# Score matmuls over 40 instead of 26 columns, and loads tied to the mixing, in talking-heads attention with an MLP

## The chip, the cores and the metric

One core of one Trainium2 chip runs the whole program. The metric is the device time of one execution in microseconds. The kernel before took 931.24 us, the median of three runs (928.26 to 932.08).

## The reference

Attention whose heads are mixed before and after the softmax, then a two-layer MLP with a PReLU (4 batches, 12 heads, 448 positions, 64 per head; 768 to 2048 to 768). q, k, v, w_pre and w_post are float32; the MLP's weights are float64.

```python
scores = scale * np.matmul(q, k.transpose(0, 1, 3, 2))
scores = np.einsum('bhij,hg->bgij', scores, w_pre)
scores = scores - np.max(scores, axis=-1, keepdims=True)
attn = np.exp(scores)
attn = attn / (np.sum(attn, axis=-1, keepdims=True) + 1e-09)
attn = np.einsum('bhij,hg->bgij', attn, w_post)
x = np.matmul(attn, v)                       # then [B*S, H*D]
h = x @ w_in
g = np.maximum(h, 0.0) + alpha * np.minimum(h, 0.0)
out = g @ w_out
```

## The kernel before

**Tiles.** Each batch's 448 query positions are cut into four chunks, three of 120 rows and one of 90 (CHUNKS, line 27); there are 16 chunks. The scores of one chunk and one pair of heads are a group Q (function qk, line 278): for two heads, hf, and two halves of the rows, ch, a matmul with at most 64 query rows as the stationary operand and k's 448 positions as the moving one. The first half has 64 columns of q, the second the rest: 56 in a 120-row chunk, 26 in a 90-row one (line 285). Each float32 matmul is two TensorE instructions in the trace, so a group Q is eight. ACT or DVE copies the result to st (qk_out, line 295).

The head mixing needs heads on partitions. A relay (line 303) is a DMA inside the on-chip memory that gathers 10 query rows times 12 heads of st into one of eight sr buffers. Two relays make a mixing block m (mix, line 308; 90 blocks in all): M mixes on TensorE, R takes the maximum on DVE (line 318), E the exponential on ACT (line 325), N the reciprocal and the scaled weights on DVE (lines 331 to 335), P the second mixing with a transpose on TensorE (line 347), A copies to at (line 359). When a chunk's blocks are done, pv (line 362) multiplies by v, xe takes the result's two parts and store_x writes them to DRAM for the MLP.

Meanwhile the raw float64 weights of the first three blocks of the MLP are fetched (fetch, line 406; six fetches of 768 KB) and rounded by seven DVE operations each (round_f64, lines 57 to 63). The MLP (lines 534 to 594) follows, two matmul layers of TensorE work, and converts the rest of its weights on the way.

**Order.** The program's order in the attention phase is written by a planner, plan (line 66). It knows every step with an engine, a duration, a priority on the scale of the mixing blocks, steps that must come before it, buffers that it takes and gives back, and sometimes an earliest time (at). It walks through them as a list scheduler would, and the instructions are written in the order of the times it assigns (line 641). A predecessor in the planner thus adds no wait to the program; it moves the instruction's place in its engine's queue. The waits in the program come from the data and the buffers alone.

**Queues.** The loads of q (LQ, load_q, line 257), k (LK, load_k, line 249; a third of a batch's k each), v (LV, load_v, line 266) and raw weights (F) are issued by GpSimd, except for the first chunk's. Relays go in turn to SP and GpSimd. GpSimd executes its queue in order, so a load stands behind the relays written before it and ahead of those after it. There are three q buffers, four for thirds of k, one for v, two for raw weights; in the planner LQ takes a buffer when one is free, and the bare earliest times of 18 and 20 hold back v and the raw weights at the start. The steps that the planner places, and their priorities, are lines 82 to 145; its costs stand in line 42 (a group Q is 0.82 whatever the chunk).

Of the kernel before, what the change touches and what calls it, by code (L numbers as in the profile page):

```python
# [31 lines left out]
NP = H // 2  # L32
# [3 lines left out]
RAHEAD = 3  # L36
# [2 lines left out]
FGROUPS = [[0, 1, 2], [3, 4, 5], [6, 7, 8], [9, 10, 11], [12, 13, 14, 15]]  # L39
NPRE = 3  # L40
NXS = 3
COST = {"Q": 0.82, "M": 0.82, "P": 1.0, "V": 2.15, "U": 3.7, "mode": 0.15, "R": 1.09, "E": 1.37, "N": 0.68}
HOP, DRAIN = 0.07, 0.2
LOOK = 0.3
# [21 lines left out]
def plan(groups, first, chunk_list):  # L66
# [5 lines left out]
    def op(name, engs, prio, preds=(), acq=(), rel=(), at=0.0):  # L72
        if isinstance(engs, tuple):
            engs = [engs]
        ops[name] = (engs, prio, list(dict.fromkeys(preds)), acq, rel, at)

    pe = lambda kind, mode="q": ("PE", COST[kind], DRAIN, mode)
    act = lambda d: ("ACT", d, HOP, "")
    dve = lambda d: ("DVE", d, HOP, "")
    dma = lambda d, l=3.0: ("DMA", d, l, "")  # L80

    for ci, (b, c) in enumerate(chunk_list):
        op(("LQ", ci), dma(1.0) if ci >= 2 else dma(0.0, 0.0), first[max(ci - 1, 0)] / 2 - RAHEAD - 5, acq=(("q", ci),))
        for p in range(NP):
            n = ci * NP + p
            prio = (n - NP) * 0.92 - 1
            op(("Q", ci, p), pe("Q"), prio, [("LQ", ci), ("LK", b, p // 2)], (("slot", (ci, p)),) + ((("st", ci),) if p == 0 else ()),
               ((("q", ci),) if p == NP - 1 else ()) + ((("k", b, p // 2),) if c == len(CHUNKS) - 1 and p % 2 else ()),
               at=5.5 + 1.1 * p if ci == 0 else 10.0)
            op(("S", ci, p), [act(0.92), dve(1.09)], prio, [("Q", ci, p)], rel=(("slot", (ci, p)),))  # L90
    for b in range(B):
        f4 = first[4 * b]
        for kk in range(NP // 2):
            op(("LK", b, kk), dma(1.2) if b else dma(0.0, 0.0), f4 / 2 - RAHEAD - 11 + kk, acq=(("k", b, kk),))
        op(("LV", b), dma(3.0), f4 / 2 + (4 if b else 0), acq=(("v", b),), at=18.0)
    for n, (ci, r) in enumerate(groups):
        op(("L", n), dma(0.8, 4.0), n / 2 - 1 - RAHEAD, [("S", ci, p) for p in range(NP)], (("sr", n),),
           (("st", ci),) if n + 1 == first[ci + 1] else ())
# [1 line left out]
    for m in range(NB):  # L100
        op(("M", m), pe("M"), m - 1, [("L", 2 * m), ("L", 2 * m + 1)], (("slot", m),), (("sr", 2 * m), ("sr", 2 * m + 1)), at=12.0)
        op(("R", m), dve(COST["R"]), m - 1, [("M", m)])
        op(("E", m), act(COST["E"]), m, [("R", m)], (("e", m),), (("slot", m),))
        op(("N", m), dve(COST["N"]), m + 1, [("E", m)], (("r", m),))
        op(("P", m), pe("P"), m + 2, [("N", m)], (("pa", m),), (("e", m), ("r", m)))
        for g in range(2):
            ci = groups[2 * m + g][0]
            op(("A", m, g), [act(0.52), dve(0.63)], m + 1.7, [("P", m)],
               (("at", ci),) if 2 * m + g == first[ci] else (), (("pa", m),))
    for ci, (b, c) in enumerate(chunk_list):  # L110
        lb = (first[ci + 1] - 1) // 2
        mine = [("A",) + divmod(n, 2) for n in range(first[ci], first[ci + 1])]
        for hx in range(2):
            pr = lb + 3.3 + 1.5 * hx
# [5 lines left out]
    nh = 2 * NPRE  # L120
    for i in range(nh):
        pr = 6 + 11 * i
        op(("F", i), dma(2.0, 4.0), pr - 6, acq=(("cr", i),), at=20.0)
        for j in range(7):
            op(("C", i, j), dve((0.57, 0.57, 0.57, 0.96, 0.57, 0.96, 0.96)[j]), pr + 1.3 * j,
               [("C", i, j - 1) if j else ("F", i)] + ([("C", i - 1, 6)] if i and not j else []),
               (("ct", i),) if j == 1 else (), (("cr", i),) if j == 5 else ())
        op(("WS", i), dma(1.0), pr + 10, [("C", i, 6)], rel=(("ct", i),))
# [3 lines left out]
    for f in range(NPRE):  # L132
        op(("LW", f), dma(2.0, 6.0), NB - 9 + f, [("WS", i) for i in range(nh)], (("cr", ("w", f)),))
        for x in range(2):
            pr = NB - 3 + 1.2 * f + 0.6 * x
# [3 lines left out]
    for u in range(2):  # L139
# [6 lines left out]

    cap = {"slot": 3, "st": NXS, "sr": 2 * (RAHEAD + 1), "e": LAG + 1, "r": LAG + 1, "pa": 1, "at": 2, "q": 3, "k": 4, "v": 1,
           "xe": 2, "cr": 2, "ct": 2}
# [14 lines left out]
    while ready:  # L163
        best = None
        for n in ready:
            engs, prio, preds, acq, rel, at = ops[n]
# [3 lines left out]
            for e, d, l, md in engs:  # L170
                d += COST["mode"] if e == "PE" and md != mode else 0.0
                t = max(t0, idle[e])
# [26 lines left out]
def talking_heads_prelu(ctx: ExitStack, tc: tile.TileContext, q, k, v, w_pre, w_post, mask, w_in, w_out, alpha, out):  # L199
    nc = tc.nc  # L200
# [5 lines left out]
    groups, first = [], []  # L206
# [40 lines left out]
    k_t, q_t, v_t, s_t, a_t = {}, {}, {}, {}, {}  # L247
# [9 lines left out]
    def load_q(ci, dmas=None):  # L257
        b, c = chunk_list[ci]
        c0, cn = CHUNKS[c]
        q_t[ci] = qp.tile([128, NP * CW], F32, tag="q", name=f"q{ci}")  # L260
        for hf in range(2):
            dma = dmas[hf] if dmas else nc.gpsimd
            dma.dma_start(out=q_t[ci][64 * hf:64 * hf + 64, :NP * cn],
                          in_=q[b, :, QOFF[c] + NP * hf * cn:QOFF[c] + NP * (hf + 1) * cn])
# [10 lines left out]
    def slot_tile(i, name):  # L275
        return ps.tile([128, 2, 512], F32, tag=f"b{i}", name=name)

    def qk(ci, p, slot):
        b, c = chunk_list[ci]
        cn = CHUNKS[c][1]  # L280
        ps = slot_tile(slot, f"s{ci}_{p}")
        for hf in range(2):
            for ch in range(2):
                r = slice(64 * hf, 64 * hf + 64)
                i0, i1 = 64 * ch, min(64 * ch + 64, cn)
                nc.tensor.matmul(ps[i0:i1, hf, :S], q_t[ci][r, p * cn + i0:p * cn + i1], k_t[b, p // 2][r, p % 2, :],  # L286
                                 start=True, stop=True)
        u_t["qk", ci, p] = ps
# [132 lines left out]
    with tc.manual_schedule():  # L421
        start = p1r.enter_context(tc.tile_pool(name="start", bufs=1, side="right"))
        hw = (nc.sync, nc.scalar)
        load_q(0, hw)
        load_k(0, 0, ((0, 1), (1, 2)), hw)
        load_k(0, 1, dmas=hw)
# [20 lines left out]
        for i, w in enumerate((w_pre, w_post)):  # L447
            for p in ((SR0, 64), (0, 64))[i]:
                nc.gpsimd.dma_start(out=mask_sb[p:p + HP, i], in_=mask[:HP, :HI, :])
                nc.gpsimd.dma_start(out=wb[p:p + HP, i, :],  # L450
                                    in_=w.rearrange("(o h) g -> o h g", o=1).to_broadcast([HI, H, H]))
        load_q(1)
        nc.gpsimd.dma_start(out=alpha_sb, in_=alpha)
        nc.vector.tensor_scalar(out=oma, in0=alpha_sb, scalar1=-1.0, scalar2=1.0, op0=ALU.mult, op1=ALU.add)
# [8 lines left out]
            op=ALU.mult,  # L463
# [14 lines left out]
        def load_x(bl, i):  # L478
            x_t[bl] = s_tile(i, f"x{len(x_log)}_{bl}").rearrange("p (t c) s -> p t c s", t=2)
            x_log.append(bl)  # L480
            x_in[i] = bl
            for t in range(2):
                nc.sync.dma_start(out=x_t[bl][:, t], in_=x2[t, :, :, bl * S:(bl + 1) * S].rearrange("c p i -> p c i"))
# [132 lines left out]
        def emit(n, e, got):  # L616
            kind, a = n[0], n[1:]
            if (kind == "LQ" and a[0] < 2) or (kind == "LK" and a[0] == 0):
                return
            if kind == "Q":  # L620
                qk(*a, got["slot"])
                if a[1] == 0:
                    s_t[a[0]] = s_tile(got["st"], f"st{a[0]}")
            elif kind in ("S", "A", "XH", "XL"):
                {"S": qk_out, "A": post_out, "XH": lambda c, x, e: pv_out(c, x, 0, e),
                 "XL": lambda c, x, e: pv_out(c, x, 1, e)}[kind](*a, e)
            elif kind == "L":
                relay_q(a[0], got["sr"])
            elif kind == "E":
                exp(a[0], 0)  # L630
                exp(a[0], 1)
            elif kind in ("M", "V", "U"):
                {"M": mix, "V": pv, "U": l1}[kind](*a, got["slot"])
            elif kind == "LX":
                load_x(a[0], got["st"])
            else:
                {"LQ": load_q, "LK": load_k, "LV": load_v, "R": rmax, "N": norm, "P": post, "W": store_x, "F": fetch,
                 "C": conv_op, "WS": store_w, "OPEN": turn, "LW": load_pre, "G": act_op,
                 "HH": lambda f, x: split_pre(f, x, 0), "HL": lambda f, x: split_pre(f, x, 1)}[kind](*a)

        for _, _, n, e, got in plan(groups, first, chunk_list):
            emit(n, e, got)
# [23 lines left out]
        def prefetch(u):  # L666
            nxt = []
            for _, bl, _ in units[u:]:
                if bl not in nxt:
                    nxt.append(bl)  # L670
                if len(nxt) == NXS:
                    break
            for bl in nxt[1:]:
                if bl not in x_in.values():
                    free = [i for i in range(NXS) if x_in.get(i) not in nxt]
                    load_x(bl, free[0])
# [54 lines left out]
```

## Time and profile before

| | |
|---|---|
| median of three runs | 931.24 us |
| the profiled execution | 935.73 us, span 934.0 us |
| TensorE matmuls | 878.8 us busy, 94% |
| DVE | 578.4 us, 62% |
| ACT | 343.5 us, 37% |
| GpSimd | 110.6 us, 12% |
| attention phase | about 0 to 440 us |
| MLP | about 440 to 934 us |

The engine shares are means over two phases with different limits. The chain that ended last is followed back from the last instruction; its pieces tell at each moment which engine or transfer the end waited for. A line like "64*26 64x448" names a stationary operand of 64 partitions and 26 columns and a moving operand of 448 columns.

### The profile page before, as it was taken

How to read it: one execution, taken by the hardware profiler on the slowest of the kernel's cores; microseconds unless marked ns; L12 is line 12 of the kernel's file. 1: busy time of each engine (PE TensorE's matmuls, PEld its weight loads, DVE VectorE, ACT ScalarE, POOL GpSimd, SP SyncE). 2: the span in 40 equal slices, each digit the busy share in tenths (PEclk: the TensorE clock that was granted, in tenths of full speed). 3: DMA queues.
4: the chain of work that ended last, by engine and by line, in shares of the span. 5: the costliest groups of instructions: out<-in, count | busy, mean ns of one | idle time of the engine just before them, and what ended most of it. 6: DMA issues, size and time to landing. Idle time of an engine off the chain costs nothing.

```text
span 934.0 us, 23852 instructions
## 1 busy us (share of the span) xinstructions
PE 878.8 (94%) x10380; PEld 665.5 (71%) x10380; DVE 578.4 (62%) x1023; ACT 343.5 (37%) x718; POOL 110.6 (12%) x194
## 2 busy tenths in 40 slices
PE   8589998999889997998899999999999999979998
PEld 3354565456553665456899999999999999869997
DVE  4475787569854886456455566667666763873332
ACT  3453765357643675346222222121212211211110
POOL 5122223222311222000000000000000000000000
PEclk9799999999999999999999999999999999989999
DMA  7666677566754469754831242025012511232111
GB/s 194 188 191 154 185 220 205 157 197 181 217 156 129 137 204 251 225 175 131 259 151 34 68 151 70 34 68 185 35 34 68 186 34 35 68 106 106 60 60 59
DMA packets 70974, 125.36 MB, mean 134 GB/s; under 512 B 32614, under 2 KB 59246, under 8 KB 70870
## 3 DMA queue, kind: packets, MB, share of 16 engines
q0 software_dynamic: 15344, 59.22, 21.8%
q1 hardware_dynamic: 54866, 63.33, 21.4%
q8 instruction: 81, 1.33, 0.6%
q10 hardware_dynamic: 660, 1.30, 0.5%
q14 instruction: 23, 0.19, 0.1%
HBM read 66.16 MB, written 18.92 MB: 91 GB/s over the span
## 4 chain that ended last, share of the span: by engine, by line
PE 82%; DVE 6%; DMA 6%; ACT 3%; issue 2%; SPq 0%; POOL 0%; ACTq 0%; DVEq 0%; POOLq 0%
PE h L541 25%; PE acc L579 24%; PE s L286 13%; PE x L369 8%; PE pa L347 7%; PE m L313 7%; DMA sr<-st 5%; DVE at L359 1%; DVE nm L318 1%; ACT e L325 1%; DVE ao L591 1%; ACT st L299 1%; ACT at L359 1%; DMA k<-in_k_dram 1%; DVE ct L60 0%
## 5 line engine op out<-in xcount | busy, mean ns | idle before, releaser
L541 PE MATMUL h<-x,w 128*128 128x448 f32 x1152 | 250.5, 370 | 6.4 <-ACT w L504 6.3
L579 PE MATMUL acc<-g,w 128*128 128x448 f32 x1152 | 245.6, 366 | 2.0 <-DVE t L556 1.4
L541 PEld LDWEIGHTS h<-x,w 128*128 128x128 f32 x1152 | 217.3, 189 | 28.8 <-ACT w L504 6.7
L579 PEld LDWEIGHTS acc<-g,w 128*128 128x128 f32 x1152 | 216.1, 188 | 21.7 <-DVE t L556 1.7
L286 PE MATMUL s<-k,q 64*64 64x448 f32 (+2 forms) x768 | 159.9, 555 | 1.9 <-ACT st L299 0.6
L347 PEld LDWEIGHTS pa<-r,e 64*64 64x64 f32 x5040 | 100.0, 136 | 58.7 <-issue 33.2
L556 DVE SCALAR_TENSOR_TENSOR t<-t,oma,h 128x448 f32<-128x448 f32 x64 | 43.5, 680 | 157.8 <-ACT t L554 157.8
L554 ACT ACTIVATE t<-h 128x448 f32<-128x448 f32 x64 | 34.9, 545 | 268.1 <-PE h L541 268.1
L325 ACT ACTIVATE e<-m,nm 128x448 f32<-128x448 f32 x180 | 112.7, 636 | 31.6 <-DVE nm L318 20.4
L318 DVE TENSOR_REDUCE nm<-m 128x2 f32<-128x896 f32 x90 | 97.6, 1085 | 36.1 <-PE m L313 35.7
L347 PE MATMUL pa<-r,e 64*64 64x60 f32 x5040 | 105.8, 223 | 14.6 <-issue 9.4
L313 PE MATMUL m<-sr,wk 64*64 64x448 f32 x720 | 97.7, 566 | 21.6 <-DMA sr<-st 18.4
L286 PEld LDWEIGHTS s<-k,q 64*64 64x64 f32 (+2 forms) x768 | 37.2, 128 | 78.2 <-issue 65.0
L369 PEld LDWEIGHTS x<-at,v 128*64 128x64 f32 x1536 | 75.6, 138 | 20.1 <-issue 6.6
L359 DVE COPY at<-pa 128x480 f32<-128x480 f32 x83 | 53.8, 656 | 54.8 <-ACT at L359 30.4
L306 POOL DMA_DIRECT2D sr<-st x89 | 53.2, 600 | 286.2 <-PE m L313 189.6
L369 PE MATMUL x<-at,v 128*64 128x120 f32 (+1 forms) x1536 | 82.5, 264 | 3.7 <-DVE at L359 1.4
L299 ACT COPY st<-s 120x896 f32<-120x896 f32 (+1 forms) x65 | 58.6, 906 | 67.7 <-PE s L286 61.2
L359 ACT COPY at<-pa 128x480 f32<-128x480 f32 x97 | 53.8, 570 | 69.7 <-PE pa L347 55.1
L313 PEld LDWEIGHTS m<-sr,wk 64*64 64x64 f32 (+1 forms) x720 | 24.9, 134 | 55.1 <-DMA sr<-st 22.2
L558 ACT CAST g<-t 128x448 fp32r<-128x448 f32 x64 | 36.3, 567 | 53.9 <-DVE t L556 53.9
L591 DVE TENSOR_TENSOR ao<-ao,acc 128x448 f32<-128x448 f32 x96 | 52.7, 613 | 1.7 <-PE acc L579 1.7
(49 smaller groups left out, 522.3 us busy)
## 6 DMA issues: line engine op xcount, KB each, us to landing
x<-x SPq DMA_DIRECT2D x16, 1344.0 KB
sr<-st SPq DMA_DIRECT2D x89, 210.0 KB
sr<-st POOLq DMA_DIRECT2D x89, 210.0 KB, 4.8
cr<-in_w_in_dram POOLq DMA_DIRECT2D x16, 768.0 KB, 4.7
cr<-in_w_out_dram POOLq DMA_DIRECT2D x16, 768.0 KB, 4.6
x<-xe SPq DMA_DIRECT2D x48, 180.0 KB
out_dram<-ao SPq DMA_DIRECT2D x24, 224.0 KB
v<-in_v_dram POOLq DMA_DIRECT2D x4, 1152.0 KB, 9.3
```

The costliest lines, as they stand in the source:

```text
L286: nc.tensor.matmul(ps[i0:i1, hf, :S], q_t[ci][r, p * cn + i0:p * cn + i1], k_t[b, p // 2][r, p % 2, :], start=True, stop=True)
L299: copy(dst[:cn, p], u_t.pop(("qk", ci, p))[:cn, :, :S])
L306: dma.dma_start(out=sr_t[n][SR0:SR0 + GP], in_=s_t[ci][r:CHUNKS[chunk_list[ci][1]][1]:CHUNKS[chunk_list[ci][1]][1] // GI])
L313: nc.tensor.matmul(ps[hf:hf + 64, u, :S], wk[r, :], g[r, :], start=True, stop=True)
L318: nc.vector.tensor_reduce(out=nm, in_=m_t[m][:, :, :S], axis=AX.X, op=ALU.max, negate=True)
L325: nc.scalar.activation(out=e_t[m][:, u], in_=m_t[m][:, u, :S], func=AF.Exp, bias=nm_t[m][:, u:u + 1], scale=1.0, accum_out=se_t[m][:, u:u ...
L347: nc.tensor.matmul(dst[:, :, HI * u:HI * u + HI], e[h, u, 64 * jb:64 * jb + 64], r[h, u].rearrange("p (h i) -> p h i", h=H), start=True, s ...
L359: copy_on[eng](dst, pa[:, g, :NS * GP].rearrange("p (s i) -> p s i", i=GI))
L369: nc.tensor.matmul(ps[64 * t:64 * t + 64, 0, cl * CW:cl * CW + cn], v_t[b][:, s, h * D:(h + 1) * D], a_t[ci][:, s, h, :cn], start=(s == 0) ...
L541: nc.tensor.matmul(ps[:, :S], w[:, tw, cc * 128:(cc + 1) * 128], x[:, tx, cc, :], start=(i == 0), stop=(i == 3 * NCC - 1))
L579: nc.tensor.matmul(accs[c][:, :S], w[:, tw, c * 128:(c + 1) * 128], g[:, tg], start=(f == fs[0] and i == 0), stop=(f == fs[-1] and i == 2))
L591: nc.vector.tensor_tensor(acc_sb[c, bl], acc_sb[c, bl], accs[c][:, :S], ALU.add)
```

## The change

The second half of a 90-row chunk's score matmuls takes 40 columns of q instead of 26 (MIN_M): rows 64 to 103 of the result instead of 64 to 89. The extra 14 columns are the next pair's first ones, and for the last pair columns of the q tile that no load fills, so a memset on GpSimd sets them to zero before the load. Rows 90 to 103 of the result are not read.

The planner's steps LQ (from chunk 2), LK (from batch 1), LV and F get a mixing block as predecessor: for LQ of chunks 2 and 3 block 0 and 1, later the block ten before the first of the preceding chunk; for LK the block fifteen (and less by one for each third) before the first of the batch; for LV the second after the batch's first; for F number i block 3 + 11 i. The earliest times of LV and F go.

```diff
+MIN_M = 40
     for ci, (b, c) in enumerate(chunk_list):
-        op(("LQ", ci), dma(1.0) if ci >= 2 else dma(0.0, 0.0), first[max(ci - 1, 0)] / 2 - RAHEAD - 5, acq=(("q", ci),))
+        op(("LQ", ci), dma(1.0) if ci >= 2 else dma(0.0, 0.0), first[max(ci - 1, 0)] / 2 - RAHEAD - 5,
+           [("M", first[ci - 1] // 2 - RAHEAD - 7)] if ci > 3 else [("M", ci - 2)] if ci >= 2 else [], acq=(("q", ci),))
...
         for kk in range(NP // 2):
-            op(("LK", b, kk), dma(1.2) if b else dma(0.0, 0.0), f4 / 2 - RAHEAD - 11 + kk, acq=(("k", b, kk),))
-        op(("LV", b), dma(3.0), f4 / 2 + (4 if b else 0), acq=(("v", b),), at=18.0)
+            op(("LK", b, kk), dma(1.2) if b else dma(0.0, 0.0), f4 / 2 - RAHEAD - 11 + kk,
+               [("M", f4 // 2 - RAHEAD - 12 + kk)] if b else [], acq=(("k", b, kk),))
+        op(("LV", b), dma(3.0), f4 / 2 + (4 if b else 0), [("M", f4 // 2 + 2)], acq=(("v", b),))
...
         pr = 6 + 11 * i
-        op(("F", i), dma(2.0, 4.0), pr - 6, acq=(("cr", i),), at=20.0)
+        op(("F", i), dma(2.0, 4.0), pr - 6, [("M", pr - 3)], acq=(("cr", i),))
...
         q_t[ci] = qp.tile([128, NP * CW], F32, tag="q", name=f"q{ci}")
+        pad = 64 + MIN_M - cn
+        if pad > 0:
+            nc.gpsimd.memset(q_t[ci][:, NP * cn:NP * cn + pad], 0.0)
...
                 r = slice(64 * hf, 64 * hf + 64)
-                i0, i1 = 64 * ch, min(64 * ch + 64, cn)
+                i0, i1 = 64 * ch, 64 * ch + 64 if not ch else max(cn, 64 + MIN_M)
                 nc.tensor.matmul(ps[i0:i1, hf, :S], q_t[ci][r, p * cn + i0:p * cn + i1], k_t[b, p // 2][r, p % 2, :],
                                  start=True, stop=True)
```

## Rows read from the trace of the kernel before

**Rows 1.** Two phases: start, end, length, busy by engine (instructions), clock, DMA share, GB/s.
```profile
0.00:440.00 440.00, 398.14 (x7926) 227.76 (x7927) 289.16 (x571) 241.41 (x545) 96.72 (x168) 0.98 0.64 184
440.00:934.00 494.00, 480.65 (x2456) 437.72 (x2454) 289.20 (x453) 102.08 (x173) 13.85 (x26) 0.99 0.26 90
```

**Rows 2.** Chain of waits in the second stretch: start, length, what; seventh chunk's scores.
```profile
178.84 3.37 PE s L286 x8
182.21 0.91 PE m L313 x8
183.12 3.35 PE s L286 x8
```

**Rows 3.** Chain of waits at a 120-row chunk: a score group.
```profile
99.02 0.75 PE s L286 x8
```

**Rows 4.** Groups by form, line 286: busy, mean ns of one, idle before.
```profile
L286 PE MATMUL s<-k,q 64*64 64x448 f32 x384 | 114.2, 554 | 1.9 <-ACT st L299 0.6 <-ACT e L325 0.5 <-DVE xe L385 0.3
...
L286 PE MATMUL s<-k,q 64*56 64x448 f32 x288 | 69.2, 558 | 0.0
...
L286 PE MATMUL s<-k,q 64*26 64x448 f32 x96 | 44.7, 545 | 0.0
...
L286 PEld LDWEIGHTS s<-k,q 64*56 64x56 f32 x288 | 17.6, 129 | 5.7 <-issue 5.1
...
L286 PEld LDWEIGHTS s<-k,q 64*26 64x26 f32 x96 | 6.0, 99 | 33.8 <-issue 33.8
```

**Rows 5.** The four stretches of 90-row scores, columns as in the first group.
```profile
66.80:97.19 30.39, 30.39 (x356) 11.08 (x357) 15.24 (x30) 11.73 (x26) 5.67 (x11) 1.00 0.62 166
166.60:196.85 30.25, 30.25 (x357) 11.02 (x357) 15.74 (x33) 11.86 (x26) 5.97 (x10) 1.00 0.58 167
272.39:302.75 30.36, 30.36 (x356) 11.09 (x359) 15.18 (x27) 11.31 (x26) 5.14 (x10) 1.00 0.51 143
372.32:405.48 33.16, 33.16 (x404) 13.61 (x405) 14.33 (x28) 11.31 (x26) 2.30 (x4) 1.00 0.57 179
sum 124.16, PE 124.16 PEld 46.81 DVE 60.49 ACT 46.21 POOL 19.09; mean PE 31.04 PEld 11.70 DVE 15.12 ACT 11.55 POOL 4.77
```

**Rows 6.** Sum over the stretches between them: 95 to 165, 200 to 271, 306 to 371.
```profile
sum 206.00, PE 187.91 PEld 122.70 DVE 162.37 ACT 135.56 POOL 48.81; mean PE 62.64 PEld 40.90 DVE 54.12 ACT 45.19 POOL 16.27
```

**Rows 7.** Three windows of the opening, columns as in the first group.
```profile
24.00:33.00 9.00, 1.12 (x12) 0.34 (x14) 1.61 (x4) 2.37 (x8) 0.65 (x1) 0.67 0.85 255
33.00:40.00 7.00, 6.88 (x140) 4.17 (x144) 5.16 (x12) 3.10 (x8) 2.15 (x4) 0.70 0.21 67
...
48.00:60.00 12.00, 10.26 (x260) 6.74 (x256) 11.34 (x26) 6.58 (x18) 2.73 (x5) 1.00 0.77 223
```

**Rows 8.** GpSimd in order of time: start, length, line, operation [idle before].
```profile
0.35 0.11 POOL L718 MEMSET const-uint8-127<- 128x1 uint8 x1
...
11.67 1.03 POOL L254 DMA_DIRECT2D k<-in_k_dram  x2 [0.28 <-DMA wb<-in_w_post_dram]
...
17.74 0.73 POOL L269 MEMSET v<- 64x768 f32 x1
18.42 0.80 POOL L270 DMA_DIRECT2D v<-in_v_dram  x1
...
19.76 0.57 POOL L397 DMA_DIRECT2D cr<-in_w_in_dram  x1
```

**Rows 9.** Chain of waits in the opening: the longest piece.
```profile
16.63 16.19 DMA sr<-st
```

**Rows 10.** TensorE's waits, 0 to 60 us: total, times, longest.
```profile
PE m L313 <- DMA sr<-st: 11.9, 6, 6.8
```

**Rows 11.** Chain of waits at the v loads of batches 1 and 2.
```profile
148.38 9.39 DMA sr<-st
...
252.92 11.64 DMA sr<-st
```

**Rows 12.** GpSimd's waits in the attention phase: total, times, longest.
```profile
POOL sr L306 <- PE m L313: 189.6, 48, 12.8
```

## The prediction

> **What bounds the kernel now.** I read the shares by phase first, then the chain of waits, then the forms of the score matmuls, then the engines by stretch. The span has two phases of nearly equal length [rows 1]: attention up to 440 us, where TensorE is busy 398 us and DVE and ACT are at 66% and 55%, and the MLP after it, with TensorE at 97%. No line that the diff touches runs in the MLP, so I leave its 494 us as they are.
>
> In the chain of the attention phase four stretches stand out in which every piece is TensorE work, back to back, and one piece recurs: eight score instructions that take 3.36 us [rows 2]. They are the six score groups (one for each p) of a 90-row chunk; two of them stand there around a mixing block of 0.91 us. The same eight instructions of a 120-row chunk take 0.75 us [rows 3], and a dozen other such pieces lie within 0.1 us of that. The forms tell the two apart [rows 4]: a single instruction lasts 545 to 558 ns whether its stationary operand has 64, 56 or 26 columns. Eight of them in 0.75 us must run side by side; 3.36 us is four pairs of 0.84 us, one pair after the other. So the 26-column pairs cost not by their own length but because nothing overlaps at the step from 64 columns to 26 and back. All stretches between the long groups are TensorE's; a shorter group there shortens the end until another engine takes over.
>
> **The score groups, part 1.** There are 24 such groups (96 instructions with 26 columns, four to a group [rows 4]). Their chain pieces in the four stretches add up to 81.7 us, 3.40 each. At 0.75 us they would be 18.0 us: **-63.7 us** of TensorE time. The trace has no form of 40 columns; the price of a group lies between 0.75 and 3.36 us. By distance 40 is no nearer to 56 than to 26. I take 0.75, because groups that mix 64 with 56 columns lose nothing [rows 3, 4]: it isn't the change of the number as such that costs, but of a class of sizes, and an array that is halved to 64 is halved next to 32, which puts 40 with 56 and 26 apart. The 14 more columns lengthen a weight load by between 0 and 30 ns (99 ns for 26, 129 for 56), 96 times, at most 2.9 us, beside matmuls of 0.54 us. I cost it at nothing; uncovered it would be the 2.9.
>
> Here a rule speaks against widening. The Trainium skill, TensorEngine Tiling (Array Packing), section Tiling Modes, gives a stationary operand of at most 32 columns a column tiling of 4 where 64 columns get 2, so by that table alone the 26-column pairs should be the cheap ones and 40 columns would win nothing; the sum would be that of the second rival below. The same section, under Key Properties, says that changing the tiling mode (not just the tile) drains the engine. The 3.36 us beside 0.75 us show what the second sentence says and not the first.
>
> **What the four stretches give back.** They last 124.2 us with TensorE at 100%; without the 63.7 us its work there is 60.5 us. DVE has 60.5 us of work in the same stretches [rows 5], so it would be as full as TensorE. In the three long stretches between them TensorE works 187.9 of 206 us, 91%, with DVE at 79% [rows 6]. At 91% the four would take 66.3 us. The nearest row with DVE that full is 48 to 60 us, where DVE is at 95% and TensorE at 86% [rows 7]; by it they take 70.8 us. I take that: **+10.3 us**. The ends: 0 if all fits, and a DMA end. The stretches hold 70.7 us of DMA time (share times length [rows 5]: 18.8 + 17.5 + 15.5 + 18.9 = 70.7); at 0.85, the fullest window [rows 7], that needs 83.2 us, +22.7.
>
> **The ties, part 2.** They only change the order in which the planner writes the instructions; most of what they move sits in GpSimd's queue, in front of or behind its half of the relays. SP's relays go past them but share the engines.
>
> The opening. Before the first blocks could be mixed, k of batch 1, v (1344 KB) and the first raw weights (768 KB) were issued [rows 8], beside a relay on SP's queue that landed after 16.2 us [rows 9]; TensorE waited 6.8 us for it before the fourth block, and 11.9 us for relays in the first 60 us [rows 10]. With the ties, v stands behind block 2, the raw weights behind block 3 and k of batch 1 behind block 7, so the first eight relays go alone with q. The bytes of v and the raw weights still pass: 2.16 MB at 223 to 255 GB/s [rows 7] are 8.5 to 9.7 us, now beside the relays of blocks 4 to 7. What is won is time in which the engines now idle: 33 to 40 us has a DMA share of 0.21 after one of 0.85 [rows 7], so 7 us x 0.64 / 0.85 = 5.3 us of transfer, and the 448 KB of k that leave the opening, 2.1 us. **-7 us**, between 0 and -11.9.
>
> Later batches. v of batches 1 to 3 needs the one v buffer, free only after the last pv of the batch before, which the planner puts at about block 27 for batch 1; a tie to block 24 is then met already. The 9.4 us wait for a relay behind v of batch 1 stays, as does the 11.6 us of batch 2 [rows 11]. k's first third of batches 2 and 3 moves from a batch ahead to blocks 30 and 52, which is where those v loads run. 448 KB at 223 GB/s are 2.1 us, twice; half of it on the path: **+2 us**, between 0 and +4.2. The raw weights move by some four blocks and q by about three; each still lands blocks ahead of its reader, at nothing; the cover is those blocks, and the third rival prices its loss.
>
> The pad. Four memsets of 14 columns on GpSimd, each between the 0.11 us of one column and the 0.73 us of 768 [rows 8]; I take 0.11. Behind each are its q loads and the later relays in that queue. The memset waits for the q buffer, for which those loads waited anyway. Four at 0.11 are 0.4 us on an engine that waits far longer for mixing [rows 12]: nothing, and at most 2.9 us uncovered.
>
> **Sum.** -63.7 + 10.3 - 7 + 2 = -58.4 us. The profiled execution lasted 935.7 us (934.0 of span), 4.5 above the median of 931.24; from it 877.3, and from the median **872.8**.
>
> **Rivals.** First, the DMA engines or the relays take over: the relays of a 90-row chunk and the k loads of the next batch come at the pace of 83.2 us for the four stretches, and the opening gains nothing since the bytes only move. -63.7 + 22.7 + 2 = -39.0: **892**. For it speak the long waits for relays wherever v is loaded [rows 11]; against it the 36% of DMA time that is free over the whole phase [rows 1]. Chance 0.12.
>
> Second, the change doesn't do what it says: at 40 columns the pairs still run one by one. Then only the opening and the k loads count, -7 + 2: **926**. For it: no row shows 40 columns; against it, 56 and 64 alike. Chance 0.03.
>
> Third, slower. The raw weights are now fetched only three blocks before their conversion's due block, in a queue whose relays wait up to 12.8 us for a mixing block [rows 12]. The conversion's instructions have fixed places in DVE's queue; if the fetch is late, the maxima and norms behind them wait, and with them ACT and TensorE. There are six fetches in this phase; six waits of 12.8 us are 76.8 us, and -58.4 + 76.8 is +18.4: **950**. It outweighs the gain from 9.7 us of lateness per fetch on. Against it: in the trace no DVE instruction waits for these fetches. Chance 0.02.
>
> Fourth, everything fits: nothing is given back in the stretches and the opening's 11.9 us go entirely, -75.6 us: **856**. Chance 0.13. The forecast itself, 864 to 884, has 0.70.
>
> **How the numbers follow.** The range runs from the fourth case, 856, to near the first, 890, and leaves out its upper half, the second and third cases and a little below: under 2 in 10. About 0.5% is what a measurement of this kernel can tell from no change, 926.6 to 935.9. All cases but the third are below it, the second barely: faster 0.96, same 0.02, slower 0.02.
>
> **What the profile after would show.** Score groups of 90-row chunks at 0.75 to 0.8 us in the chain; the fourth block's 6.8 us wait for a relay gone; the attention phase ended by about 382 us; DVE and DMA shares of that phase at 75% or more; the MLP within 2 us of what it was. Groups still at 3.4 us would make the first term wrong. DMA waits before mixing blocks above some 30 us in total on TensorE would show the first rival, a DVE wait for raw weights the third.

## The result and the profile after

The changed kernel took 886.56 us, the median of four runs (884.24 to 896.11), against 931.66 us before: a ratio of 0.953, 95% interval 0.943 to 0.962. Timed once more with more rounds it gave 0.957 (0.953 to 0.961). The profiled execution lasted 884.75 us, 51.0 less than that of before. The gain is large and of the announced kind, but some 13 us short of the forecast's 58.4. Ratios here and below leave out slowed executions, the longest of them 2773 us in the experiment with q and k tied.

The two phases, columns as in [rows 1]:

```profile
0.00:390.00 390.00, 340.17 (x7924) 221.49 (x7924) 287.73 (x569) 239.94 (x546) 96.53 (x172) 0.96 0.74 207
390.00:883.00 493.00, 480.83 (x2462) 438.68 (x2458) 289.62 (x453) 102.40 (x174) 13.80 (x26) 0.99 0.26 90
```

The MLP is what it was. The attention phase is 50 us shorter, TensorE's busy time in it 58 us less, and the DMA share has risen from 0.64 to 0.74.

The score instructions of the narrow form, the row that answers to the 64\*26 row of [rows 4]:

```profile
L292 PE MATMUL s<-k,q 64*40 64x448 f32 x96 | 22.3, 545 | 0.0
```

One instruction still lasts 545 ns; as a group the 96 are busy 22.3 us instead of 44.7, so they overlap with their neighbours. In the chain of waits such a group is now two pieces, 0.82 us together, against 0.75 for a 120-row chunk [rows 3]:

```profile
160.18 0.06 PE s L292 x2
...
160.25 0.76 PE s L292 x6
```

The stretches of 90-row scores, columns as in [rows 5]; the windows are about those of blocks 12 to 17, 33 to 39, 56 to 62 and 78 to 84:

```profile
69.10:91.50 22.40, 20.49 (x482) 13.46 (x478) 18.01 (x38) 16.89 (x39) 6.74 (x12) 1.00 0.88 233
151.10:175.40 24.30, 22.62 (x599) 15.39 (x595) 20.35 (x42) 15.96 (x38) 7.45 (x13) 1.00 0.87 236
249.00:273.50 24.50, 19.75 (x490) 13.27 (x487) 17.79 (x33) 13.59 (x32) 7.45 (x13) 1.00 0.91 235
339.80:363.30 23.50, 20.96 (x526) 14.19 (x520) 16.82 (x34) 13.41 (x32) 3.45 (x6) 1.00 0.88 277
```

TensorE was at 100% here with a DMA share of 0.51 to 0.62 [rows 5]; now the share is 0.87 to 0.91, DVE is at 72 to 84%, and TensorE has gaps. What it waits for, in the whole attention phase (total, times, longest):

```profile
PE pa L353 <- issue: 18.7, 13, 2.7
PE m L319 <- DMA sr<-st: 13.8, 7, 3.3
PE pa L353 <- DVE at L365: 4.5, 5, 1.4
PE pa L353 <- DVE r L341: 2.3, 4, 0.9
```

The waits for DVE are short. "issue" is a wait that no semaphore in the profile explains; before, it was half of that:

```profile
PE pa L347 <- issue: 9.4, 6, 3.0
```

To find where the time went I counted mixing blocks, numbered from 0: the start of each block's last mixing instruction (eight to a block), and its difference to the kernel before. This is worked out from the trace's instructions, one profiled execution each. "Untied" is the kernel with the 40 columns and without the ties; it and the other columns are the experiments below.

```
block    before    minus before, us:
         us        after  untied  ties only  ties vf  ties qk  f free  k free  opening
   3      36.5      -2.1   -2.0     -1.3      -6.0     +1.3    -0.2    -3.5    -2.1
   9      53.6      +3.2   -0.8     +2.0      +1.8     +5.1    -1.4    -0.2    +2.0
  18     106.2     -15.1  -10.5     -2.5     -10.0     +3.2    -7.7   -15.0   -17.4
  27     140.3     -14.3  -11.2     -1.7      -9.1     +3.3    -8.5   -14.1   -16.2
  33     165.1     -14.1  -11.3     -1.7      -8.8     +2.0    -9.2   -15.5   -17.3
  42     212.8     -27.7  -25.5     -1.7     -22.7    -11.7   -21.0   -26.6   -30.8
  51     248.6     -27.5  -26.4     +0.2     -22.2    -12.5   -20.6   -26.1   -31.8
  54     265.0     -24.1  -26.3     +3.0     -21.9     -8.5   -19.4   -25.9   -30.9
  60     303.1     -39.9  -43.0     +1.4     -37.9    -25.8   -35.3   -42.4   -47.2
  63     316.1     -35.8  -42.9     +1.4     -36.0    -24.1   -33.9   -38.4   -47.4
  75     359.4     -35.8  -42.9     +1.4     -36.0    -24.1   -33.9   -38.4   -47.4
  87     422.4     -50.5  -56.1     +1.1     -49.8    -31.3   -47.4   -52.4   -61.3
  89     429.2     -49.5  -55.7     +3.0     -48.5    -31.4   -46.0   -51.6   -60.3
```

The gain of the changed kernel comes in four steps, one a batch (blocks 9 to 18, 33 to 42, 54 to 63, 75 to 87): 18.3, 13.6, 11.7 and 14.7 us, 58.3 together. In the opening it falls 3.2 us behind, between blocks 51 and 54 it loses 3.4, and within the third step, at blocks 60 to 63, 4.1 of what it had won.

Two more profiles have the same order of instructions: the changed kernel's second timing and the kernel with 33 columns. At blocks 51 to 54 they lose 2.7 and 4.3 us, at 60 to 63 3.6 and 4.2, so these two losses come again. The one in the opening does not: at block 9 they stand at -0.3 and +0.6 instead of +3.2. A difference of some 3 us in the opening of one profile is therefore not more than one kernel differs from itself.

### The profile page after: what moved, and what is told of

Its sections match the earlier page's. It is cut to its first block, busy times and chain, and to the rows that moved or that the text cites. A ratio compares the mean times of both kernels' runs of the same rounds, so it can differ in the third digit from the quotient of the medians.

```text
span 882.8 us, 23839 instructions
## 1 busy us (share of the span) xinstructions
PE 821.0 (93%) x10380; PEld 660.2 (75%) x10380; DVE 577.3 (65%) x1022; ACT 342.3 (39%) x719; POOL 110.3 (12%) x198
## 4 chain that ended last, share of the span: by engine, by line
PE 77%; DMA 7%; DVE 7%; ACT 4%; issue 3%; POOL 1%; ACTq 0%; DVEq 0%; POOLq 0%
PE h L547 26%; PE acc L585 25%; PE x L375 8%; PE pa L353 7%; PE m L319 6%; DMA sr<-st 6%; PE s L292 5%; DVE at L365 1%; ACT e L331 1%; DVE nm L324 1%; ACT at L365 1%; DMA x<-xe 1%; ACT st L305 1%; DVE ao L597 1%; DMA q<-in_q_dram 1%
## 5 line engine op out<-in xcount | busy, mean ns | idle before, releaser
L353 PE MATMUL pa<-r,e 64*64 64x60 f32 x5040 | 108.5, 225 | 26.5 <-issue 18.7
L319 PE MATMUL m<-sr,wk 64*64 64x448 f32 (+1 forms) x720 | 102.1, 576 | 17.5 <-DMA sr<-st 13.8
L324 DVE TENSOR_REDUCE nm<-m 128x2 f32<-128x896 f32 x90 | 97.7, 1085 | 26.1 <-PE m L319 25.8
L292 PE MATMUL s<-k,q 64*64 64x448 f32 (+2 forms) x768 | 100.8, 560 | 2.1 <-ACT st L305 0.7
L312 POOL DMA_DIRECT2D sr<-st x89 | 53.4, 603 | 259.3 <-PE m L319 158.1
L305 ACT COPY st<-s 120x896 f32<-120x896 f32 (+1 forms) x65 | 58.4, 905 | 31.3 <-PE s L292 29.6
L319 PEld LDWEIGHTS m<-sr,wk 64*64 64x64 f32 (+1 forms) x720 | 27.6, 137 | 48.7 <-issue 20.0
L566 DVE TENSOR_TENSOR g<-t,g 128x448 fp32r<-128x448 f32 x64 | 39.9, 623 | 14.7 <-ACT g L564 14.7
```

The costliest lines, as they stand in the source:

```text
L305: copy(dst[:cn, p], u_t.pop(("qk", ci, p))[:cn, :, :S])
L312: dma.dma_start(out=sr_t[n][SR0:SR0 + GP], in_=s_t[ci][r:CHUNKS[chunk_list[ci][1]][1]:CHUNKS[chunk_list[ci][1]][1] // GI])
L319: nc.tensor.matmul(ps[hf:hf + 64, u, :S], wk[r, :], g[r, :], start=True, stop=True)
L324: nc.vector.tensor_reduce(out=nm, in_=m_t[m][:, :, :S], axis=AX.X, op=ALU.max, negate=True)
L353: nc.tensor.matmul(dst[:, :, HI * u:HI * u + HI], e[h, u, 64 * jb:64 * jb + 64], r[h, u].rearrange("p (h i) -> p h i", h=H), start=True, s ...
```

## Experiments

The theory on record was that the columns give about 53 us and the ties 5 more. After the block times a theory B stood beside it (the ties give nothing), then D: the ties gather loads in places where others run, and cost time; and at last E: the burst of v's load costs time by itself. Only the kernel with v of batch 0 throughout leaves something out.

### The two parts apart

The columns without the ties: the four planner lines of the diff as in the kernel before.

```diff
-        op(("LV", b), dma(3.0), f4 / 2 + (4 if b else 0), [("M", f4 // 2 + 2)], acq=(("v", b),))
+        op(("LV", b), dma(3.0), f4 / 2 + (4 if b else 0), acq=(("v", b),), at=18.0)
```

(and likewise LQ, LK and F)

> The 40 columns and the pad alone, the loads placed as in the kernel before. Prediction on record: columns -63.7 + 10.3 = -53, so about 878 from 931, and the ties worth another -5 beyond that. Theory B, from the block times of the changed kernel (four stretches gain 12 to 18 us each, the opening loses 3): the ties give nothing, 880 to 890, equal to the changed kernel within 0.7%. Rival C: the faster score groups need the ties, because k, q and raw weights would collide with the relays; then 895 or more.

Ratio 0.940 (0.933 to 0.947), median 877.7 us. That is better than theory B and what the prediction had for the columns (about 878): the columns alone are ahead of the whole change. Their gain in the profile is 55.7 us at the last block; in the four steps 9.7, 14.2, 16.6 and 13.2, together 53.7, where the prediction had -63.7 + 10.3 = -53.4.

The ties without the columns: MIN_M's two places as before.

```diff
-                i0, i1 = 64 * ch, 64 * ch + 64 if not ch else max(cn, 64 + MIN_M)
+                i0, i1 = 64 * ch, min(64 * ch + 64, cn)
```

> The ties alone, 26 columns as before. Prediction on record: -7 + 2, 926. Theory B: the bytes of v and raw weights only move from before to behind the first four blocks, 929 to 935. Rival C has no effect here, since the slow score groups leave time: 926 to 931.

Ratio 1.005 (1.001 to 1.009): half a percent slower, not the 5 us faster of the prediction. The opening's longest wait for a relay is shorter (3.6 instead of 6.8 us), but block 9 comes 2.0 us late, and 2.8 us are lost between blocks 51 and 54 even here, where slow score groups leave the engines time.

The relay in the opening's chain of waits, in the kernel with the ties alone:

```profile
17.83 10.69 DMA sr<-st
```

Before it took 16.19 us [rows 9], with v and the raw weights beside it. Without them it still takes 10.7. And with them, in the untied kernel, the relay that the chain names takes no longer:

```profile
18.08 10.47 DMA sr<-st
```

### Which columns

32 and 33 instead of 40:

```diff
-MIN_M = 40
+MIN_M = 32
```

> The changed kernel with 32 instead of 40 columns. If a stationary operand of up to 32 columns is of the narrower class, the groups stay at 3.4 us and the time is that of the ties alone, 930 to 938. If the cost had come from an odd number of columns or from the rows that follow, it would be near 886.

> The changed kernel with 33 columns. If the class boundary lies at 32, one column more gives the whole gain: groups at 0.75 us, 884 to 890. If the cost fell gradually with the columns, it would lie between.

934.2 us and 886.6 us, one execution each. The forms and one group of 90-row scores in each chain, first 32 columns, then 33:

```profile
L292 PE MATMUL s<-k,q 64*32 64x448 f32 x96 | 44.9, 548 | 0.0
...
172.99 3.37 PE s L292 x8
```

```profile
L292 PE MATMUL s<-k,q 64*33 64x448 f32 x96 | 22.6, 550 | 0.0
...
148.53 0.06 PE s L292 x2
...
148.60 0.76 PE s L292 x6
```

One column more takes a group from 3.37 to 0.82 us. The step lies between 32 and 33; the number of columns beyond it costs nothing that these rows show. The Trainium skill, TensorEngine Tiling (Array Packing), section Tiling Modes, lists tiles of 64 and of 32 columns and says that a change of mode drains the engine; the trace agrees with a boundary at 32, and shows that pairs on its two sides don't overlap, though not by itself that this is a drain. The table under Theoretical Speedup, in the Overview of that page of the Trainium skill, gives a dimension of at most 32 up to 4 times the speed and one of at most 64 up to 2 times; no gain of the narrower tile shows in these rows, in which a pair of the other class stands between any two narrow ones. Narrow pairs one behind the other, which would change class less often, were not run.

### Which ties

v and raw weights tied, q and k as before:

```diff
-           [("M", first[ci - 1] // 2 - RAHEAD - 7)] if ci > 3 else [("M", ci - 2)] if ci >= 2 else [], acq=(("q", ci),))
+           acq=(("q", ci),))
...
-               [("M", f4 // 2 - RAHEAD - 12 + kk)] if b else [], acq=(("k", b, kk),))
+               acq=(("k", b, kk),))
```

> 40 columns, v and raw weights tied, q and k as before. If what the ties do is in the opening (v, raw weights), this equals the changed kernel, 884 to 888; if q and k matter (moved into v's bursts at blocks 30 and 52), it is 2 to 4 us faster than the changed kernel: 882 to 885.

Ratio 0.952 (0.945 to 0.959), 886.5 us: as the changed kernel. It does not lose between blocks 51 and 54, as expected of k's old place, but it loses 1.9 us at 60 to 63 and was 5 us behind the changed kernel by block 27. The expected 2 to 4 us did not come against the first timing.

q and k tied, v and raw weights as before:

```diff
-        op(("LV", b), dma(3.0), f4 / 2 + (4 if b else 0), [("M", f4 // 2 + 2)], acq=(("v", b),))
+        op(("LV", b), dma(3.0), f4 / 2 + (4 if b else 0), acq=(("v", b),), at=18.0)
...
-        op(("F", i), dma(2.0, 4.0), pr - 6, [("M", pr - 3)], acq=(("cr", i),))
+        op(("F", i), dma(2.0, 4.0), pr - 6, acq=(("cr", i),), at=20.0)
```

> 40 columns, q and k tied, v and raw weights with their earliest times as before. By the prediction it loses the 5 us that the opening's v and raw weights were to give: 878 to 892. By theory B it equals the changed kernel within 3 us, with the fourth block later by some 5 us and the tenth earlier by 3.

Ratio 0.962 (0.954 to 0.970), outside of what either theory gave. The first 27 blocks are lost almost whole: q of chunk 2, tied to block 0, is now issued at 18.1 us, together with v (19.9) and the raw weights (21.2), and k, q and raw weights follow each other again at 84 to 87 us. Which of these bursts costs what is not shown: the untied kernel has a similar one at 73 to 76 us and gains. The granted clock, too, was at its lower level for 27 us of the first 105, in four stretches, against 13.7 us in one in the changed kernel.

The changed kernel without the tie of the raw weights, and without that of k (the same lines alone):

> The changed kernel with the tie of the raw weights alone undone. Theory D (the ties gather loads where others run: raw weights of block 58 beside k and q, and TensorE's waits without a visible cause at 257, 264 and 271 us follow): blocks 60 to 63 gain 2 to 4 us against the changed kernel and those waits shrink; in the opening v alone is behind block 2. Total 881 to 885. Rival: the position of the raw weights is indifferent and the differences between the kernels so far are chance; 885 to 889.

Ratio 0.958 (0.953 to 0.964), 895.1 us: not faster in total, against the expectation, and right in the place it named. Blocks 60 to 63 lose 1.4 us instead of 4.1; but the first raw weights come at 18.9 us again, and at block 27 it is 5.8 us behind the changed kernel.

> The changed kernel with the tie of k alone undone, so k's first third comes a batch ahead again and not with v of batches 2 and 3. Theory D: the 3.4 us lost between blocks 51 and 54 go, total 882 to 885; the prediction on record priced this at 2 us for two batches. Rival: a relay waits for v alone, k beside it costs nothing; the step stays, 885 to 889.

Ratio 0.952 (0.946 to 0.959), 885.8 us. The loss between blocks 51 and 54 is gone (-26.1 to -25.9), as theory D wanted; the one at 60 to 63 stays (4.0 us), and the time is just above the expected range, in the rival's, and not under the changed kernel's first timing by more than its spread.

What stands at those two places. Blocks 51 to 54 in the changed kernel, GpSimd's queue, and the chain's piece there, then the piece of the untied kernel:

```profile
219.50 0.79 POOL L276 DMA_DIRECT2D v<-in_v_dram  x1
...
225.57 1.09 POOL L257 DMA_DIRECT2D k<-in_k_dram  x2
...
224.95 15.55 DMA sr<-st
```

```profile
226.48 11.79 DMA sr<-st
```

Before the relay took 11.64 us behind v alone [rows 11]; with 448 KB of k beside it 15.6, and 15.0 in the kernel with 33 columns, which has the same order.

Blocks 57 to 63 in the changed kernel, GpSimd's queue and the chain, then the only wait of its kind in the untied kernel:

```profile
253.13 1.10 POOL L257 DMA_DIRECT2D k<-in_k_dram  x2 [1.14 <-PE s L292]
...
256.45 1.07 POOL L257 DMA_DIRECT2D k<-in_k_dram  x2 [1.57 <-PE s L292]
257.51 0.56 POOL L403 DMA_DIRECT2D cr<-in_w_out_dram  x1
...
262.23 1.06 POOL L269 DMA_DIRECT2D q<-in_q_dram  x2
...
257.56 1.19 issue
...
264.36 1.57 issue
...
271.46 1.99 issue
```

```profile
255.14 0.56 issue
```

The tie of the last raw weights to block 58 puts 768 KB beside two thirds of k; q of the next chunk, tied to a later block too, follows 4.7 us later. TensorE then stands still three times, 4.75 us, with no semaphore to wait for; two of the three, 3.6 us, lie between blocks 60 and 63. In the two other profiles of the same order the loss at this place has another form: the chain goes through a relay, here in the second timing and with 33 columns:

```profile
258.60 10.38 DMA sr<-st
```

```profile
258.95 11.01 DMA sr<-st
```

So the place and the size come again, and not what TensorE is seen to wait for. In the untied kernel the raw weights are issued at block 48 and q at block 56, and one wait of 0.56 us is left. The losses at blocks 60 to 63 go with what is there besides k: 0.1 (nothing more), 1.9 with raw weights (ties vf), 1.4 and 1.7 with q (f free, ties qk), 4.0 to 4.1 with both (k free, after).

### The ties for the opening alone

```diff
-           [("M", first[ci - 1] // 2 - RAHEAD - 7)] if ci > 3 else [("M", ci - 2)] if ci >= 2 else [], acq=(("q", ci),))
+           [("M", ci - 2)] if ci in (2, 3) else [], acq=(("q", ci),))
...
-               [("M", f4 // 2 - RAHEAD - 12 + kk)] if b else [], acq=(("k", b, kk),))
+               [("M", 7)] if b == 1 and kk == 0 else [], acq=(("k", b, kk),))
...
-        op(("F", i), dma(2.0, 4.0), pr - 6, [("M", pr - 3)], acq=(("cr", i),))
+        op(("F", i), dma(2.0, 4.0), pr - 6, [] if i else [("M", 3)], acq=(("cr", i),), at=20.0)
```

> 40 columns, and the ties kept for the opening alone: q of chunks 2 and 3, the first third of k of batch 1, v, and the first raw weights; everything later placed as in the kernel before. Theory D: the changed kernel leads the untied one by 3 us at block 27 and loses 3.4 at blocks 51 to 54 and 4 at 60 to 63; with the opening's part of the ties alone it should lead at block 27 and lose neither: 872 to 878, 0 to 5 us under the untied kernel. Rival: the opening's lead is chance or is given back; 878 to 886.

Ratio 0.942 (0.938 to 0.946), 878.4 us; the profiled execution, 873.85 us, is the shortest profiled one. Its blocks do what theory D says: 2 us ahead of the changed kernel's first profile at block 27 (level with the second), then a loss of 0.9 between 51 and 54 and none at 60 to 63. In time it equals the untied kernel; the 5 us of lead at block 27 that its profile has over that one are not seen in the medians.

The changed kernel's own interval touched that of this one, so it was timed again:

> The changed kernel itself, timed again with more rounds, since its interval (0.943 to 0.962) touches those of the two kernels without the later ties (0.933 to 0.947 and 0.938 to 0.946). Theory D, the later ties cost 6 us or more: ratio 0.947 to 0.957. Rival, the difference between the kernels is the spread of their runs: 0.940 to 0.946.

0.957 (0.953 to 0.961) against 0.942 (0.938 to 0.946). The later ties cost about 10 us by the first timing and 14 by the second, 1.1 to 1.5%. The profiled executions differ by 11, of which the table places 3.4 - 0.9 = 2.5 us at blocks 51 to 54, 4.3 at 60 to 63 and 2 before block 27; the rest of the medians' difference I can't place. The executions of the changed kernel had a mean granted clock of 0.969 to 0.978 in the second timing, those of the kernel with the opening's ties 0.975 to 0.988; whether the ties cause the lower clock no run shows.

The two timings of the same kernel, 0.953 and 0.957, also say what the single experiments above can tell: against the second, the kernel without the tie of the raw weights (0.958) is no slower, and those without the tie of k, or with v and the raw weights tied (both 0.952), may be some 4 us faster. What is known of single ties is known from the blocks.

### What v's burst costs

v of batch 0 for all batches, on the changed kernel: three loads of 1344 KB are left out, and the output is that of other values of v.

```diff
+        if b:
+            v_t[b] = v_t[0]
+            return
```

> The changed kernel with v of batch 0 used for all batches: three loads of 1344 KB are left out. It prices v's bursts. Theory E: the waits without a visible cause and those for relays at blocks 30, 53 and 76 go, together 8 to 15 us: 872 to 879. Rival: the chunk's relays alone make the DMA engines full there, 883 to 887.

873.9 us in one execution, 10.9 below the changed kernel's profiled execution. By the block times 5.0 us come back between blocks 27 and 33 and 10.4 between 51 and 54, where v of batches 1 and 2 was loaded; 1.6 are lost again at 60 to 63, and between 75 and 87 another 2.6. TensorE's waits (total, times, longest), to compare with those of the changed kernel above:

```profile
PE m L322 <- DMA sr<-st: 12.3, 4, 4.5
PE pa L356 <- issue: 6.9, 6, 1.8
PE pa L356 <- DVE at L368: 4.7, 6, 1.4
PE x L378 <- issue: 2.9, 2, 2.3
```

The waits for relays are hardly fewer; those named issue before P fall from 18.7 to 6.9 us. Theory E was right in the time and for these waits, and wrong for the relays.

v in six buffers of 128 positions, on the untied kernel, two quarters loaded before the batch begins:

```diff
-        op(("LV", b), dma(3.0), f4 / 2 + (4 if b else 0), acq=(("v", b),), at=18.0)
+        for s in range(NS):
+            m = (0, 2, 4, 5)[s] if not b else f4 // 2 + (-4, -1, 2, 2)[s]
+            op(("LV", b, s), dma(0.8), m + 1, [("M", m)], acq=(("v", b, s),))
```

> The untied kernel with 40 columns, v kept in six buffers of 128 positions each instead of one of 448, two of a batch's four loaded some five and two blocks before the batch begins, the other two where all of v came before. Theory E: v's single burst of 1344 KB costs 2 to 4 us a batch (waits for relays, for instructions, and the low clock after them); with 576 KB there, half of it goes: 872 to 877. Rival: the bytes only move to other relays, 877 to 882.

Ratio 0.942 (0.935 to 0.949): no different from the untied kernel. Its runs spread from 873.6 to 893.3 us and the profiled one was the longest, so its blocks are not read. Spreading v's bytes over the blocks before gave nothing that this measurement can tell; the 10.9 us came back where the bytes were left out.

## Why the prediction was right, and where its steps were not

**The score groups** were right in cause and nearly in size. Groups fell to 0.82 us, the busy time of the score matmuls by 59.1 us (159.9 to 100.8), and TensorE's busy time in the phase by 58 (forecast 63.7; mixing instructions run a little longer on average, 576 against 566 ns, with the mean clock of the phase at 0.96 against 0.98). The reading that 40 columns belong with 56 was the one that no row of before could show; 32 against 33 settles it.

**What the stretches give back.** The sum of the first two terms, -53.4, met the 53.7 gained by the untied kernel, in part by luck: its score matmuls were busy 60.6 us less (159.9 to 99.3), 3 less than forecast, and so 6.9 us were given back instead of 10.3. The engine that fills the stretches is not the one I named. I took DVE's fullness as the nearest row; in the trace DVE is at 72 to 84%, TensorE waits 6.8 us for it in the whole phase, and the DMA share is 0.87 to 0.91. As far as these shares tell, the first rival had the resource right; that the DMA engines set the pace there was not tested. Its price, 83.2 us for four stretches at 0.85, was too high, because these transfers go on at more than 0.85.

**The opening** was the first wrong step. I took the 16.2 us of a relay as the price of v and raw weights beside it. The wait for it, 6.76 us, also stood in the middle of the third block (number 2) and not before the fourth, as the kernel before shows:

```profile
25.12 0.98 PE L313 MATMUL m<-sr,wk 64*64 64x448 f32 x8 [1.37 <-DMA sr<-st]
32.87 1.01 PE L313 MATMUL m<-sr,wk 64*64 64x448 f32 x2 [6.76 <-DMA sr<-st]
```

Without these loads the relay that the chain names takes 9.7 us:

```profile
17.99 9.73 DMA sr<-st
...
53.33 2.74 issue
```

Eight relays of 210 KB and one q of 360 KB are 2.1 MB, 9.4 us at the 221 GB/s that went over the DMA engines from 18 to 28 us; most of the wait was their own. Block 3 came 2.1 us earlier, not 7, and even these 2.1 need not be the ties': in the untied kernel, with v and raw weights where they were, it came 2.0 us earlier. What the ties can claim are TensorE's waits for relays in the first 60 us (total, times, longest), in the untied kernel and the changed one, against 11.9 us before [rows 10]:

```profile
PE m L317 <- DMA sr<-st: 8.5, 5, 5.0
```

```profile
PE m L319 <- DMA sr<-st: 6.0, 2, 3.3
```

The deferred v (31.1 us) and raw weights (32.5 us) then met the relays of the following blocks, q and k; block 9 came 3.2 us late in this profile, after the 2.74 us wait at 53.33, though not in the two others of the same order. That the bytes only move stood in my first rival, with the wrong conclusion for the sum. Later the order pays off a little: at block 27 the changed kernel leads the untied one by 3.1 us, by 5.0 in its second profile.

**k** moved into v's burst was right in mechanism and place: a loss of 3.4 us at blocks 51 to 54, forecast 2 for two batches; for k of batch 2, at block 30, it cost nothing that can be seen (0.2 us from block 27 to 33); there k was issued 13 us after v, and not 6.

**The raw weights and q**, "at nothing", was the second wrong step, and the same mistake in another form. I looked for the reader that could be late, found blocks of cover, and stopped. No reader was late: no DVE instruction waits for a raw weight in the changed kernel, and the third rival did not come. What was hit were the relays, or waits of TensorE that no semaphore explains, at the place where k already ran: 4 us at blocks 60 to 63.

**The sum.** -58.4 forecast, -45 in the first medians and about -40 in the second. The columns gave 55.7 in the profile and a ratio of 0.940; the ties, forecast at -5, cost 6 us by the profiles and 9 to 15 by the timings. The time lay inside the range since this was bounded by the DMA price, not because the forecast's middle was right. Of the signs named in advance, the score groups and the MLP came as said, and the 6.8 us wait for a relay is gone (the longest in the opening is now 3.3 us, before the first block); the phase ended at 390 us and not 382, with DVE and DMA at 74%.

## What to carry to other kernels

A group of score matmuls in which stationary operands of 26 or 32 columns alternate with 64 took 3.36 us here, against 0.82 with 33 or 40; filling them up with columns that nobody reads is free as far as these rows show. Once the engine that hid them is faster, transfers that never showed begin to show: before moving a load, ask not only whether its reader can wait, but what else is on the DMA engines at the place it moves to. Time a changed kernel twice and profile it twice before explaining differences of 3 us. And try a change's parts apart: here one part alone gave more than the whole.

## What the runs showed of the hardware

TensorE may have waited for its own instructions. The waits named issue before P are the largest group in the changed kernel (18.7 us, against 9.4 before). They go with loads, if not with the DMA share alone: 6.9 us with v's loads left out, 12.4 in the untied kernel at the same share of 0.74. In the DMA queues of the window from 52 to 57 us, around the wait at 53.33, there is one packet of instructions among the full queues:

```profile
q0 software_dynamic: 168, 0.69, 64.3%
q1 hardware_dynamic: 127, 0.20, 24.9%
q8 instruction: 1, 0.02, 1.6%
```

Each such packet is 16 KB, and 62 come in the attention phase, one about every 6 us, and 19 in the MLP. That is one packet to every 256 and 259 of TensorE's instructions (15848 and 4920, matmuls and weight loads), so the packets of this queue go with TensorE's count. All ten idle stretches of TensorE over 1 us that are put down to issue in the changed kernel begin within 1.4 us of the start of such a packet (53.20 us before the wait at 53.33, 81.03 before that at 82.1, 271.06 before that at 271.46). The nine of the second timing do so within 1.5 us, and four of the five of the kernel before; the fifth begins 0.3 us ahead of a packet. In two of the ten the packet's own record has ended when the wait begins, so what TensorE still waits for is open. That its instructions came late behind the loads fits these rows; it is read from times that coincide and was not tested by itself.

The granted clock fell to its lower level, 1.2 of 2.4 GHz, for 13.7 us in the opening of the changed kernel (10.2 before), after 6.6 us in which TensorE was busy 2.8, and then for 3.4, 6.8 and 3.4 us, each time 9 to 13 us after the load of a batch's v was issued (3.4 each before, 11 to 20 us after). In the second profile of the changed kernel the opening's 13.7 us come again, and the rest is 3.4, 6.8 and 3.4 us at other places, so the link with v's loads is not shown.
